# Attention by two pairs of heads: q times the key-value blocks in row halves of TensorE instead of against block-diagonal matrices

## The chip, the cores and the metric

The kernel runs on one core of one Trainium2 chip. The metric is the device time of one execution in microseconds. A core has five engines with their own instruction queues: PE (TensorE, matrix products), DVE (VectorE), ACT (ScalarE), POOL (GpSimd) and SP (here only issuing DMA transfers). PE reads both operands from SBUF and writes to PSUM, which has eight banks of 512 fp32 values in each of 128 partitions. A matrix product is two steps, which the profile shows as two rows: the *stationary* operand (`lhsT`) is loaded (PEld), then the *moving* operand (`rhs`) is streamed past it (PE). `lhsT` has its contraction index on the partitions, and its columns become the output's partitions. All is in fp32; each fp32 product leaves two records in each of the two rows, a transpose leaves one.

## What is computed

Attention without a softmax, normalised by head and followed by a layer of four experts:

```python
kv  = np.einsum('bhsd,bhse->bhde', k, v)          # 64 x 64 per head
out = np.einsum('bhsd,bhde->bhse', q, kv)
rms = np.sqrt(np.mean(out * out, axis=-1, keepdims=True) + 1e-06)
x   = out / rms * g_norm                           # 8 batches, 8 heads, 576 rows, 64
x   = x.transpose(0, 2, 1, 3).reshape(4608, 512)
# experts:
p = domain_probs / (domain_probs.sum(-1, keepdims=True) + 1e-09)
for e in range(4):                                 # w1: 512 x 1024, w2: 1024 x 512
    y += p[:, e:e + 1] * (np.maximum(x @ w1[e], 0.0) @ w2[e])
```

Nearly all arithmetic is in the experts; the kernel computes them by nested Strassen-like forms, which the change does not touch.

## The kernel before

The kernel is written as a plan: every operation is added with a key (where in the program it belongs), an estimated cost by engine, and the buffers it reads and writes. Ahead of time, a list scheduler in the kernel turns this into one fixed order per engine and gives each buffer a slot. So a change of one part moves the order of the others. Attention for batch b+1 is laid between the expert products of batch b, in the first of the four experts; batch 0 comes first, alone. While it runs, PE is given idle transposes of the identity (`idle`, line 1253) wherever the scheduler sees it free.

PSUM's eight banks are in four kinds of two: `u1` and `u2` (first expert product), `db` (second expert product), `ab` (attention). For batch 0, `db` serves attention too.

One batch has eight heads in four pairs. For each pair `hp` (512 of the 576 rows; the remaining 64 rows of all heads follow in one piece):

```python
        def turn(eng, bank=bank, qt=qt):            # line 590: q transposed, two heads on 128 partitions
            for r in range(NR):                     # NR = 4 blocks of 128 rows
                rs = slice(r * P, (r + 1) * P)
                nc.tensor.transpose(bank.ap[:, rs], qt.ap[:, rs], ident[:])
        ...                                         # line 595: ACT copies it to SBUF as qT
        def key_values(eng, bank=bank, kt=kt, vt=vt):   # line 605: two heads in two column halves
            for j in range(KR):                     # KR = 6 pieces of 96 rows
                for r in range(2):
                    nc.tensor.matmul(
                        bank.ap[r * D:(r + 1) * D, 0:D], lhsT=kv_rows(kt)[:, r, j, :],
                        rhs=kv_rows(vt)[:, r, j, :], start=(j == 0), stop=(j == KR - 1),
                    )

        def diagonal(eng, bank=bank, to=kvbd[hp]):  # line 613: into the diagonal of a zeroed 128x128 block
            for r in range(2):
                rows = slice(r * D, (r + 1) * D)
                nc.scalar.activation(out=to.ap[rows, rows], in_=bank.ap[rows, 0:D], func=ACT.Copy)
        ...
        def attend(eng, raw=raw, qT=qT, kb=kvbd[hp]):   # line 623: q times the block-diagonal matrix
            for r in range(NR):
                rs = slice(r * P, (r + 1) * P)
                nc.tensor.matmul(raw.ap[:, rs], lhsT=qT.ap[:, rs], rhs=kb.ap[:])

        plan.add(at(hp + 0.4), pe(4, P), attend, reads=[qT, kvbd[hp]], writes=[raw])
        x = Buf("small", f"x{n}")
        scaled(at(hp + 0.4), n, raw, P, x)
        ...
        def turn_x(eng, bank=bank, x=x):            # line 633: x transposed again, for the experts
            for r in range(NR):
                rs = slice(r * P, (r + 1) * P)
                nc.tensor.transpose(bank.ap[:, rs], x.ap[:, rs], ident[:])
        ...                                         # line 639: ACT copies it, times g_norm
```

With the block-diagonal matrix, one product of 128x128 serves two heads; half of its stationary-by-moving multiplications are with zeros. `scaled` normalises:

```python
    def scaled(key, name, raw, n, x):
        ...
        # line 528, ACT:  sq = raw ** 2                 (n x 512)
        # line 533, DVE:  ss = sum of sq by head        (n x 8)
        # line 538, POOL: ss = ss / 64 + eps
        # line 542, POOL: rt = ss ** -0.5               (n x 8)
        # line 549, DVE:  x = raw * rt                  (n x 512)
```

The remaining 64 rows go through the same steps: transposes (line 657), the product (672), `scaled`, transposes (687):

```python
        def attend_rem(eng):                        # line 672
            for hp in range(NPAIR):
                nc.tensor.matmul(
                    rawr.ap[0:REM, hp * P:(hp + 1) * P], lhsT=qTr.ap[:, hp * REM:(hp + 1) * REM],
                    rhs=kvbd[hp].ap[:],
                )
```

The helper at line 360 is used by all additions of the Strassen-like forms; line 830 is the first expert product, 1044 and 1119 the second in its plain and its deep form, 917 the first product of batch 0.

Of the kernel before, what the change touches and what calls it, by code (L numbers as in the profile page):

```python
# [230 lines left out]
def kernel(  # L231
# [58 lines left out]
    dram = ctx.enter_context(tc.tile_pool(name="dram", bufs=1, space=bass.MemoryType.DRAM))  # L290

    ident = const.tile([P, P], F32, name="ident")
    mhalf = const.tile([P, H], F32, name="mhalf")
    gcol = const.tile([P, 1], F32, name="gcol")
    p_all = const.tile([P, NBLK, E], F32, name="p_all")
    tot = const.tile([P, NBLK], F32, name="tot")
# [2 lines left out]
    BANKS = {"u1": 2, "u2": 2, "db": 2, "ab": 2}  # L299
    SHAPE = {  # L300
        "big": (29, 2 * NT), "w1y": (7, 768), "xf": (5, 2 * NT), "snap": (5, HN),
        "ss": (4, H), "rt": (4, H),
    }
    slots = {
        kind: [
# [209 lines left out]
            halves[c] = [Buf("big", f"x{c}_{dh}") for dh in range(2)]  # L515
        return halves[c]

    def scaled(key, name, raw, n, x):

        sq = Buf("small", f"sq{name}")  # L520
        ss, rt = Buf("ss", f"ss{name}"), Buf("rt", f"rt{name}")

        def rows(b):
            return b.ap[0:n, :].rearrange("p (h d) -> p h d", d=D)

        plan.add(
            key, act(NT),
            lambda eng: nc.scalar.activation(out=sq.ap[0:n, :], in_=raw.ap[0:n, :], func=ACT.Square),
            reads=[raw], writes=[sq],
        )  # L530
        plan.add(
            key, dve(NT),
            lambda eng: nc.vector.reduce_sum(out=ss.ap[0:n, :], in_=rows(sq), axis=AX.X),
            reads=[sq], writes=[ss],
        )

        def power(eng):
            nc.gpsimd.tensor_scalar(
                out=ss.ap[0:n, :], in0=ss.ap[0:n, :], scalar1=1.0 / D, scalar2=EPS,
                op0=ALU.mult, op1=ALU.add,  # L540
            )
            nc.gpsimd.tensor_tensor(
                out=rt.ap[0:n, :], in0=ss.ap[0:n, :], in1=mhalf[0:n, :], op=ALU.pow
            )

        plan.add(key - 0.3, {"POOL": 1.9}, power, reads=[ss], writes=[ss, rt])
        plan.add(
            key, dve(NT),
            lambda eng: nc.vector.tensor_tensor(
                out=rows(x), in0=rows(raw),  # L550
                in1=rt.ap[0:n, :].unsqueeze(2).to_broadcast([n, H, D]), op=ALU.mult,
            ),
            reads=[raw, rt], writes=[x],
        )

    def attention(b, key, span, rem):

        kvbd = {}
        at = lambda j: key + span * j / (NPAIR + 1)
        for hp in range(NPAIR):  # L560
            hs = slice(2 * hp, 2 * hp + 2)
            n = f"{b}_{hp}"
            kind = "kv" if b or hp < 2 else "big"
            kt, vt, qt = Buf(kind, f"k{n}"), Buf(kind, f"v{n}"), Buf("small", f"q{n}")
            want = at(hp) - 0.25 if b else key - 1 + 0.1 * hp

            def kv_rows(t):
                return t.ap[0:KP, 0:2 * KR * D].rearrange("p (h j d) -> p h j d", h=2, d=D)

            for r in range(2):  # L570
                load(
                    want, qt,
                    lambda qt=qt, r=r: qt.ap[:].rearrange(
                        "p (r h d) -> p r h d", h=2, d=D)[:, :, r, :],
                    q[b, 2 * hp + r, 0:NT, :].rearrange("(p r) d -> p r d", r=NR), 128,
                )
            for t, src in ((kt, k), (vt, v)):
                load(
                    want, t,
                    lambda t=t: t.ap[0:KP, 0:2 * KR * D].rearrange("p (h x) -> p h x", h=2),  # L580
                    src[b, hs].rearrange("h (p j) d -> p h (j d)", j=KR), 288,
                )

            bank = Buf("ab", f"qT{n}")
            qT = Buf("small", f"qT{n}")

            def turn(eng, bank=bank, qt=qt):
                for r in range(NR):
                    rs = slice(r * P, (r + 1) * P)
                    nc.tensor.transpose(bank.ap[:, rs], qt.ap[:, rs], ident[:])  # L590

            plan.add(at(hp), pe(4, P, 1), turn, reads=[qt], writes=[bank])
            plan.add(
                at(hp), act(NT),
                lambda eng, bank=bank, qT=qT: nc.scalar.activation(
                    out=qT.ap[:], in_=bank.ap[:], func=ACT.Copy),
                reads=[bank], writes=[qT],
            )
            bank = Buf("ab" if b else "ab", f"kv{n}")
            kvbd[hp] = Buf("kvbd", f"kvbd{n}")  # L600

            def key_values(eng, bank=bank, kt=kt, vt=vt):
                for j in range(KR):
                    for r in range(2):
                        nc.tensor.matmul(  # L605
                            bank.ap[r * D:(r + 1) * D, 0:D], lhsT=kv_rows(kt)[:, r, j, :],
                            rhs=kv_rows(vt)[:, r, j, :], start=(j == 0), stop=(j == KR - 1),
                        )

            def diagonal(eng, bank=bank, to=kvbd[hp]):  # L610
                for r in range(2):
                    rows = slice(r * D, (r + 1) * D)
                    nc.scalar.activation(out=to.ap[rows, rows], in_=bank.ap[rows, 0:D], func=ACT.Copy)

            plan.add(at(hp), {"PE": 0.87}, key_values, reads=[kt, vt], writes=[bank])
            plan.add(at(hp), {"ACT": 0.5}, diagonal, reads=[bank], writes=[kvbd[hp]])

            raw = Buf("ab" if b else "db", f"raw{n}")

            def attend(eng, raw=raw, qT=qT, kb=kvbd[hp]):  # L620
                for r in range(NR):
                    rs = slice(r * P, (r + 1) * P)
                    nc.tensor.matmul(raw.ap[:, rs], lhsT=qT.ap[:, rs], rhs=kb.ap[:])  # L623

            plan.add(at(hp + 0.4), pe(4, P), attend, reads=[qT, kvbd[hp]], writes=[raw])
            x = Buf("small", f"x{n}")
            scaled(at(hp + 0.4), n, raw, P, x)
            bank = Buf("ab" if b else "db", f"xT{n}")

            def turn_x(eng, bank=bank, x=x):  # L630
                for r in range(NR):
                    rs = slice(r * P, (r + 1) * P)
                    nc.tensor.transpose(bank.ap[:, rs], x.ap[:, rs], ident[:])  # L633

            plan.add(at(hp + 1), pe(4, P, 1), turn_x, reads=[x], writes=[bank])
            xh = x_halves(b)[hp // 2]
            plan.add(
                at(hp + 1), act(NT),
                lambda eng, bank=bank, xh=xh, kt=hp % 2: nc.scalar.activation(
                    out=xh.ap[:, kt * NT:(kt + 1) * NT], in_=bank.ap[:], func=ACT.Copy,  # L640
                    scale=gcol[:]),
                reads=[bank], parts=[xh],
            )

        n = f"{b}_r"
        at = lambda j: rem + 0.1 * (j - NPAIR)
# [18 lines left out]
            lambda eng: nc.scalar.activation(out=qTr.ap[:, 0:HN], in_=tb.ap[:, 0:HN], func=ACT.Copy),  # L665
            reads=[tb], writes=[qTr],
        )
        rawr = Buf("ab", f"raw{n}")

        def attend_rem(eng):  # L670
            for hp in range(NPAIR):
                nc.tensor.matmul(  # L672
                    rawr.ap[0:REM, hp * P:(hp + 1) * P], lhsT=qTr.ap[:, hp * REM:(hp + 1) * REM],
                    rhs=kvbd[hp].ap[:],
                )

        plan.add(
            at(NPAIR), pe(4, P), attend_rem, reads=[qTr] + [kvbd[hp] for hp in range(NPAIR)],
            writes=[rawr],
        )  # L680
        xr = Buf("small", f"x{n}")
        scaled(at(NPAIR), n, rawr, REM, xr)
        xb = Buf("ab", f"xT{n}")

        def turn_xrem(eng):
# [571 lines left out]
    with tc.manual_schedule(engines={ENG.PE, ENG.DVE, ENG.Activation, ENG.Pool, ENG.SP}):  # L1257
        for i in range(P // D):
            nc.sync.dma_start(out=gcol[i * D:(i + 1) * D, :], in_=g_norm.unsqueeze(1))
        make_identity(nc, ident[:])  # L1260
        nc.vector.memset(mhalf[:], -0.5)
        nc.vector.memset(bd_home[:], 0.0)
        held = None
        wide = {}
        for op in order:
            if op.seed:
                bank, n = op.marks
                assert wide.get((bank.kind, bank.slot), 0) >= n, "a seed would be overwritten"
            elif op.eng == "PE":
                for b in op.outs:  # L1270
                    wide[b.kind, b.slot] = op.marks[1] if op.marks else 0
            made = op.fn(op.eng)
            if op.port and op.eng == "DVE":
                held = made.ins.name
            elif op.port and op.eng == "POOL" and held is not None:
                tc.add_manual_dep(made.ins, held, mybir.DependencyInfo(
                    mybir.DependencyClass.Sync, mybir.DependencyReason.DATA
                ), reason="SBUF port")
# [28 lines left out]
```

## Time and profile before

The time is 1748.28 us, the median of three runs (1747.76 to 1748.77). The profiled execution spans 1747.1 us. PE's clock is granted in full throughout.

| | PE | PEld | DVE | ACT | POOL |
|---|---|---|---|---|---|
| busy, us | 1738.6 | 1664.1 | 1151.4 | 931.6 | 719.7 |
| instructions | 14222 | 14222 | 1712 | 2274 | 758 |

What attention leaves in the trace:

| line | engine | what | records | length of one, ns |
|---|---|---|---|---|
| 590, 633 | PE | transposes of q and of x, 128x128 | 128 and 128 | 272 to 273 |
| 605 | PE | keys times values, 96x64 by 96x64 | 768 | 222 |
| 623 | PE | q times the block-diagonal, 128x128 | 256 | 275 |
| 672 | PE | the same for the remaining rows | 64 | 273 |
| 1253 | PE | idle transposes at the start | 94 | 273 to 325 |
| 595 | ACT | copy of the transposed q | 32 | 597 |
| 613 | ACT | copy of a diagonal block | 64 | 219 |
| 528 | ACT | squares | 40 | 597 |
| 533 | DVE | sums by head | 40 | 685 |
| 538, 542 | POOL | scale, power | 40 and 40 | 197, 1636 |
| 549 | DVE | multiply | 40 | 690 |
| 639 | ACT | copy of x, times g_norm | 32 | 688 |

How to read it: PE's records overlap, [...]so the length of one says little of what it costs. What it costs is the distance from its start to the start of the next. A record of PEld is likewise longer than the distance to the next load.

### The profile page before, as it was taken

The page shows a single profiled execution, that of the slowest core. Times are in us where ns is not written, and L with a number is a line of the kernel's source. Part 1 is how long each engine was busy: PE and PEld are TensorE (multiplying, and loading weights), DVE is VectorE, ACT ScalarE, POOL GpSimd, SP SyncE. Part 2 cuts the span into 40 slices and gives each one's busy share as a digit, 9 for nine tenths or more (in the row PEclk, how much of TensorE's full clock was granted, in tenths as well). Part 3 has the DMA queues.
Part 4 walks back from the last instruction along what each step waited for, and adds up shares of the span by engine and source line. Part 5 has one row for each costly group of instructions (what it writes and reads, how often), then busy time and mean ns, then how long its engine had stood idle before and what let it go on. Part 6 is the DMA issues. An engine that isn't in the chain of part 4 may idle for free.

```text
span 1747.1 us, 36218 instructions
## 1 busy us (share of the span) xinstructions
PE 1738.6 (100%) x14222; PEld 1664.1 (95%) x14222; DVE 1151.4 (66%) x1712; ACT 931.6 (53%) x2274; POOL 719.7 (41%) x758
## 2 busy tenths in 40 slices
PE   9999999999999999999999999999999999999998
PEld 7699999999999999999999999999999999999997
DVE  4854554555565567777786567777787567777774
ACT  3454544554444456666555456665655446666662
POOL 2534343444233424333355624333345624333331
PEclk9999999999999999999999999999999999999999
DMA  9765444533343334444456434444456434444442
GB/s 230 237 185 180 136 144 139 147 128 119 120 146 100 103 98 110 109 109 110 122 158 156 101 94 112 107 109 110 109 158 169 109 90 108 117 108 110 107 103 49
DMA packets 148587, 220.80 MB, mean 126 GB/s; under 512 B 49600, under 2 KB 90816, under 8 KB 148416
## 3 DMA queue, kind: packets, MB, share of 16 engines
q1 hardware_dynamic: 133312, 191.21, 35.2%
q0 software_dynamic: 15104, 27.27, 11.3%
q8 instruction: 112, 1.84, 0.4%
q14 instruction: 59, 0.48, 0.1%
HBM read 145.30 MB, written 73.14 MB: 125 GB/s over the span
## 4 chain that ended last, share of the span: by engine, by line
PE 99%; DMA 0%; DVE 0%; ACT 0%; SPq 0%; issue 0%; ACTq 0%
PE u L830 44%; PE db L1044 17%; PE db L1119 16%; PE ab L1119 10%; PE ab L1044 4%; PE u L917 2%; PE ab L605 2%; PE ab L623 1%; PE ab L590 1%; PE ab L633 1%; PE ab L1253 1%; PE ab L672 0%; DMA small<-in_q_dram 0%; PE db L623 0%; PE ab L687 0%; PE ab L657 0%
## 5 line engine op out<-in xcount | busy, mean ns | idle before, releaser
L360 DVE TENSOR_TENSOR big<-big,big 128x1024 f32<-128x1024 f32 (+1 forms) x429 | 479.1, 1128 | 61.9 <-ACT big L813 33.4
L830 PE MATMUL u<-xf,big 128*128 128x128 f32 x3536 | 508.4, 275 | 0.0
L830 PEld LDWEIGHTS u<-xf,big 128*128 128x128 f32 x3536 | 455.5, 192 | 4.8 <-issue 0.9
L830 PE MATMUL u<-xf,w1y 128*128 128x128 f32 x2652 | 381.3, 275 | 0.0
L857 DVE TENSOR_TENSOR big<-u,snap 128x256 f32<-128x256 f32 x446 | 188.1, 422 | 254.6 <-PE u L830 170.9
L830 PEld LDWEIGHTS u<-xf,w1y 128*128 128x128 f32 x2652 | 342.8, 192 | 3.9
L849 ACT ACTIVATE snap<-u 128x256 f32<-128x256 f32 x490 | 187.9, 383 | 249.0 <-PE u L830 211.5
L1044 PE MATMUL db<-big,big 128*128 128x256 f32 x1192 | 280.2, 380 | 0.0
L1044 PEld LDWEIGHTS db<-big,big 128*128 128x128 f32 x1192 | 216.3, 190 | 24.5 <-issue 0.2
L849 ACT ACTIVATE big<-u 128x256 f32<-128x256 f32 x446 | 170.0, 383 | 95.7 <-PE u L830 63.0
L360 POOL TENSOR_TENSOR big<-big,big 128x256 f32<-128x256 f32 (+1 forms) x116 | 139.4, 1217 | 111.6 <-DVE big L360 75.1
L360 POOL TENSOR_TENSOR big<-big 128x512 f32<-128x512 f32 (+1 forms) x78 | 93.0, 1194 | 169.0 <-DVE big L360 120.6
L813 ACT ACTIVATE big<-big 128x1024 f32<-128x1024 f32 x124 | 130.2, 1052 | 8.8 <-DVE big L360 7.0
L1185 POOL TENSOR_TENSOR big<-big 128x512 f32<-128x512 f32 x19 | 24.1, 1270 | 217.9 <-DVE big L360 164.1
L1119 PE MATMUL db<-big,big 128*128 128x128 f32 x788 | 113.0, 275 | 0.0
L1147 ACT ACTIVATE snap<-db 128x256 f32<-128x256 f32 (+1 forms) x168 | 60.0, 357 | 94.5 <-PE db L1119 87.2
L849 ACT ACTIVATE u<-u 128x256 f32<-128x256 f32 x245 | 91.0, 372 | 25.9 <-PE u L830 10.2
L1119 PEld LDWEIGHTS db<-big,big 128*128 128x128 f32 x788 | 100.3, 192 | 0.0
L1014 POOL DMA_DIRECT2D out_dram<-big x98 | 88.3, 987 | 22.4 <-ACT big L991 16.6
L991 ACT ACTIVATE big<-db,p_all 128x256 f32<-128x256 f32 x90 | 42.6, 473 | 95.1 <-PE db L1044 93.9
L1119 PE MATMUL db<-kv,big 128*128 128x128 f32 x624 | 88.6, 275 | 0.0
L1119 PE MATMUL ab<-kv,big 128*128 128x128 f32 x588 | 84.1, 275 | 0.0
(200 smaller groups left out, 2687.1 us busy)
## 6 DMA issues: line engine op xcount, KB each, us to landing
xf<-x SPq DMA_DIRECT2D x108, 512.0 KB, 3.6
out_dram<-big POOLq DMA_DIRECT2D x82, 256.0 KB, 5.5
xf<-x_h SPq DMA_DIRECT2D x81, 256.0 KB, 3.2
xf<-x SPq DMA_DIRECT2D x81, 256.0 KB, 3.4
x<-xf SPq DMA_DIRECT2D x36, 512.0 KB, 3.3
big<-in_moe_w_dram SPq DMA_DIRECT2D x28, 512.0 KB, 4.9
small<-in_q_dram SPq DMA_DIRECT2D x72, 128.0 KB, 4.0
kv<-in_k_dram SPq DMA_DIRECT2D x30, 288.0 KB, 3.5
```

Source lines behind the costliest of these rows:

```text
L360: lambda eng: adder(eng).tensor_tensor(out=out_(), in0=a(), in1=b(), op=op),
L605: nc.tensor.matmul(bank.ap[r * D:(r + 1) * D, 0:D], lhsT=kv_rows(kt)[:, r, j, :], rhs=kv_rows(vt)[:, r, j, :], start=(j == 0), stop=(j == ...
L813: lambda eng: nc.scalar.activation(out=b.ap[:], in_=b.ap[:], func=ACT.Relu),
L830: nc.tensor.matmul(ps.ap[:, u * P:(u + 1) * P], lhsT=w1f[e][m][mm][1]()[:, u * P:(u + 1) * P], rhs=views[m][mm][1](), start=(mm in (1, 5) ...
L849: lambda eng: nc.scalar.activation(out=where(), in_=ps.ap[:, 0:HN], func=ACT.Copy),
L857: lambda eng: nc.vector.tensor_tensor(out=block(whole, a, t), in0=src.ap[:, 0:HN], in1=add_.ap[:], op=ALU.add),
L917: nc.tensor.matmul(bank.ap[:], lhsT=two(w.ap[:])[:, kt, ut * P:(ut + 1) * P], rhs=two(xh[dh].ap[:])[:, kt, :], start=(dh == kt == 0), stop ...
L991: lambda eng: nc.scalar.activation(out=cell(i, half), in_=ap(), func=ACT.Copy, scale=prob()),
L1014: nc.gpsimd.dma_start(out=dst, in_=cell(i)[parts, :], accum_op=ALU.add)
L1044: nc.tensor.matmul(ps.ap[:, 0:HN], lhsT=four(h[m])[:, kt // 2, t, kt % 2, :], rhs=w2f[e][m].ap[:, kt * HN:(kt + 1) * HN], start=(m in (1, ...
L1119: nc.tensor.matmul(ps.ap[:, o * P:(o + 1) * P], lhsT=b.ap[:, col:col + P], rhs=w2q[e][m][mm][1]()[:, kt, :], start=(mm in (1, 5) and o == ...
L1147: lambda eng: nc.scalar.activation(out=where(), in_=group_of(ps.ap), func=ACT.Copy),
```

## The change

The change takes two pairs of heads together (a group) and does without block-diagonal matrices. The key-value blocks of a group's four heads lie in one bank and are copied by one ACT instruction as they are: the two heads of a pair above each other on 128 partitions, the pairs side by side. q times a key-value block is then done head by head: a head's 64 partitions of the transposed q are the stationary operand, its 64x64 block the moving one. The even heads use the upper 64 rows of PE, the odd heads the lower 64, and each parity writes to a bank of its own (`raw[0]`, `raw[1]`). The products with zeros go. `scaled` squares and multiplies bank by bank, and sums and takes the power of both at once (16 sums a row in place of 8); its second multiply puts the heads back in their order by a strided output. The normalised rows of a group are in a buffer of 1024 columns.

```diff
-            def diagonal(eng, bank=bank, to=kvbd[hp]):
-                for r in range(2):
-                    rows = slice(r * D, (r + 1) * D)
-                    nc.scalar.activation(out=to.ap[rows, rows], in_=bank.ap[rows, 0:D], func=ACT.Copy)
...
+                def key_values(eng, bank=kbank, kt=kt, vt=vt, o=o):
+                    for j in range(KR):
+                        for r in range(2):
+                            nc.tensor.matmul(
+                                bank.ap[r * D:(r + 1) * D, o * D:(o + 1) * D],
+                                lhsT=kv_rows(kt)[:, r, j, :], rhs=kv_rows(vt)[:, r, j, :],
+                                start=(j == 0), stop=(j == KR - 1), skip_group_check=True,
+                            )
...
             plan.add(
+                at(2 * g + 1), act(P),
+                lambda eng, bank=kbank, to=kv[g]: nc.scalar.activation(
+                    out=to.ap[:], in_=bank.ap[:, 0:P], func=ACT.Copy),
+                reads=[kbank], writes=[kv[g]],
+            )
+            raw = [Buf("ab" if b > 1 else "db", f"raw{b}_{g}_{r}") for r in range(2)]
...
-            def attend(eng, raw=raw, qT=qT, kb=kvbd[hp]):
-                for r in range(NR):
-                    rs = slice(r * P, (r + 1) * P)
-                    nc.tensor.matmul(raw.ap[:, rs], lhsT=qT.ap[:, rs], rhs=kb.ap[:])
-
-            plan.add(at(hp + 0.4), pe(4, P), attend, reads=[qT, kvbd[hp]], writes=[raw])
+            def attend(eng, raw=raw, g=g):
+                for o in range(2):
+                    for i in range(NR):
+                        for r in range(2):
+                            half = slice(r * D, (r + 1) * D)
+                            nc.tensor.matmul(
+                                raw[r].ap[:, (o * NR + i) * D:(o * NR + i + 1) * D],
+                                lhsT=qTs[2 * g + o].ap[half, i * P:(i + 1) * P],
+                                rhs=kv[g].ap[half, o * D:(o + 1) * D],
+                            )
+
             plan.add(
+                at(2 * g + 1.4), {"PE": 1.0}, attend, reads=[qTs[2 * g], qTs[2 * g + 1], kv[g]],
+                writes=raw,
+            )
+            x = Buf("big", f"xg{b}_{g}")
+            scaled(at(2 * g + 1.4), f"{b}_{g}", raw, P, x, 2 * NR)
...
         def attend_rem(eng):
             for hp in range(NPAIR):
-                nc.tensor.matmul(
-                    rawr.ap[0:REM, hp * P:(hp + 1) * P], lhsT=qTr.ap[:, hp * REM:(hp + 1) * REM],
-                    rhs=kvbd[hp].ap[:],
-                )
+                for r in range(2):
+                    half = slice(r * D, (r + 1) * D)
+                    nc.tensor.matmul(
+                        rawr[r].ap[0:REM, hp * D:(hp + 1) * D],
+                        lhsT=qTr.ap[half, hp * REM:(hp + 1) * REM],
+                        rhs=kv[hp // 2].ap[half, hp % 2 * D:(hp % 2 + 1) * D],
+                    )
...
-        nc.vector.memset(bd_home[:], 0.0)
```

Not shown: `scaled`, which now runs over two banks as told above (its buffer of squares is gone; the squares go into x's own buffer), and the sizes of its small buffers (two of 16 columns in place of four of 8).

## The prediction, made before the changed kernel ran

> **What bounds the kernel now.** I read the page from the top: busy shares, then the chain of work that ended last, then the waits of PE.
>
> ```profile
> PE 1738.6 (100%) x14222; PEld 1664.1 (95%) x14222; DVE 1151.4 (66%) x1712; ACT 931.6 (53%) x2274; POOL 719.7 (41%) x758
> ...
> PE 99%; DMA 0%; DVE 0%; ACT 0%; SPq 0%; issue 0%; ACTq 0%
> ```
>
> The first line gives busy time and instruction counts by engine, the second the chain's shares of the span. PE, the matmul row, has work in 1738.6 of 1747.1 us and carries 99% of the chain; the other engines have a third of their time or more to spare. In the waits of PE only four single entries appear (1.4, 1.1, 0.8 and 0.4 us). So a change is worth what it changes in PE's own time, whatever it does for DVE, ACT or GpSimd, unless it makes PE wait.
>
> "Busy" here hides how fast matmuls follow each other: a record of a 128-column product lasts 275 ns, but the next starts long before. So the rate must be read from starts. The timeline of PE around one key-value block (start, length, engine, line, count of records):
>
> ```profile
> 155.31 0.50 PE L830 MATMUL u<-xf,big 128*128 128x128 f32 x3
> 155.74 0.92 PE L605 MATMUL ab<-kv,kv 96*64 96x64 f32 x24
> 156.59 0.46 PE L657 MATMUL ab<-ident,small 64*128 64x64 f32 x4
> 156.98 1.16 PE L830 MATMUL u<-xf,w1y 128*128 128x128 f32 x8
> 157.97 1.06 PE L623 MATMUL ab<-kvbd,small 128*128 128x128 f32 x8
> 158.87 0.38 PE L1044 MATMUL db<-big,big 128*128 128x256 f32 x1
> ```
>
> and of its weight loads (the stationary operand, lhsT):
>
> ```profile
> 155.74 0.78 PEld L605 LDWEIGHTS ab<-kv,kv 96*64 96x64 f32 x24
> ...
> 157.86 0.97 PEld L623 LDWEIGHTS ab<-kvbd,small 128*128 128x128 f32 x8
> ```
>
> Three rates come out. An fp32 matmul is two records. (a) L623, the q product that the change rewrites: 8 records from 157.97 to 158.87, 0.90 us for one pair of heads, **112 ns a record**. (b) L605, two products in two column halves of PE: 0.92 us less the 222 ns of one record, over 23 gaps, is **30 ns a record**, though each streams 64 columns; (a)'s rate would give 56. So two halves do run side by side. (c) Entering such a stretch costs: the last L830 record starts at 155.31+0.50-0.275 = 155.535, the next is 0.205 later instead of 0.11; leaving L605 takes 0.15 instead of 0.03. **About 0.1 us for each change of mode**, 0.2 for an excursion. L623 pays none of it now, since its neighbours are 128x128 too. The remainder's product L672 does:
>
> ```profile
> 161.58 1.09 PE L672 MATMUL ab<-kvbd,small 128*64 128x128 f32 x8
> 162.60 0.71 PE L830 MATMUL u<-xf,big 128*128 128x128 f32 x4
> ```
>
> It takes 1.02 us from its start to the next.
>
> [...]loads of 128 columns last 192 ns (L623), of 64 columns 138 (L605), 54 ns apart for 64 columns.[...]
>
> **The change part by part.** *The q product.* Before, two pairs of heads are 2 x 0.90 = 1.80 us, 16 times in the kernel: 28.8 us. After, two pairs are 16 products of half the rows and half the moving columns, 32 records. If the moving columns set the pace as in L605, 32 x 30 ns = 0.97 us. But L605's stationary operand has 64 columns; here it is still a q block of **128 columns**, and there are twice as many loads. [...]If the two halves load side by side, two records take about 112 ns, 16 x 0.112 = 1.79 us, plus 0.2 for the excursion: 1.99. Nothing is gained in the halving, and the excursion is lost: 16 x 0.19 = **+3.0 us**.
>
> *The remainder's q product* has 64-column weights, so L605's rate fits: 16 records x 30 ns = 0.48, plus 0.2, is 0.68 against 1.02, 8 times: **-2.7 us**.
>
> *The start.* Before the first feed-forward product PE has little to do and the program puts in idle transposes of the identity (L1253). They stand on PE's queue and take its time whether needed or not. There are 94 such records in the trace; the order of the changed program has 120, because a group of two pairs must be complete before its q product and the second group's now stands ahead of the first feed-forward product. 26 x 0.111 = **+2.9 us**.
>
> *The chain behind the q product.* For two pairs: two squares on ACT (0.60 each), a row sum of 1024 on DVE (0.69 now for 512, so about 1.2), POOL's scale (0.2) and power, two multiplies on DVE (0.69 each). The power took 1.64 us for 8 columns; 16 columns take 1.64 to 3.3. That is 5.6 to 7.3 us, some 0.4 more with hand-overs. In the changed order PE has 6.2 us of work between the first q product and the transpose that needs its result (40 records of transposes at 0.11 and two key-value blocks of 0.86), 7.8 behind the second, and over 8 from then on. So only the first can stall PE, by 0 to 1.5 us: **+0.5**.
>
> *Off the path:* eight copies of a diagonal block (0.22 us each on ACT) become two of 128 columns per batch, the row sums are fewer, the zeroing of the block-diagonal buffer (0.91 us on DVE while PE waits for q) goes. ACT, DVE and POOL are not the bound, so these are worth nothing. Key-value products, transposes and everything of the feed-forward part keep their counts, and the last 2499 rows of PE's order are the same.
>
> Sum: 3.0 - 2.7 + 2.9 + 0.5 = +3.7, so **1752 us**.
>
> **The rivals.** (1) *The moving columns set the pace after all.* Then a group is 0.97 + 0.2 = 1.17 us and the q products save 16 x 0.63 = 10.1; with -2.7 and +3.4 the sum is -9.4: 1739 us. For it: L605's rate. Against it: 54 ns of load per 64 columns; L605 cannot tell[...].
> (2) *Row halves do not load side by side.* Then each record waits for a full load, 32 x 0.11 + 0.2 = 3.7 us a group, +30 us; the remainder gains nothing (16 x 54 ns + 0.2); with the start +34: 1782 us. For it: no row half beside another in this trace. Against it: column halves do it.
> (3) *A half cannot load while it multiplies itself.* [...]L605 speaks against it.
> (4) *PSUM or the chain becomes a wait.* In the later batches a q product holds both banks of the attention pair until the second multiply, some 6 to 8 us. The eight batches stretch over some 400 us (L623 runs from 12.6 to 396.5), near 50 each, and PE has other products to go on with, so I expect no more than 2 us.
>
> **Range and chances.** I give the main case about one half, rival 1 a fifth, rivals 2 and 3 three in ten together. 1737 to 1780 holds the first, the main case and most of the others. All but the far end of rival 2 lie within 2% of 1748.28 (1713 to 1783), so "same" is nearly sure.
>
> **What would show it.** In the changed timeline: the 32 records of one q product, start to next start. 1.9 to 2.1 us confirms the load as the pace, 1.1 to 1.2 rival 1,[...] 3.5 or more rival 2. The remainder's should take about 0.7. The idle transposes should number 120 and the first feed-forward product start 1 to 3 us after 25.87. The waits of PE should stay under 5 us; a large one on the multiply or the transpose's copy would mean rival 4. The prediction is wrong if row halves share loads in a way that the column halves do not show, or if the power on 16 columns holds up more than the first group.

## The result and the profile after

The changed kernel takes 1751.77 us (1751.34 to 1752.37), against 1748.53 us for the kernel before (four runs, one more than above): 3.2 us more, a ratio of 1.0019 with a 95% interval of 1.0001 to 1.0036. The difference is small, and the interval only just excludes 1. The products with zeros, half of all in that step, are gone for nothing.

The page of the changed kernel, busy time and instructions by engine, then the chain's shares:

```profile
PE 1741.5 (100%) x14568; PEld 1663.4 (95%) x14568; DVE 1154.8 (66%) x1745; ACT 917.7 (52%) x2234; POOL 702.0 (40%) x684
...
PE 99%; DMA 0%; DVE 0%; SPq 0%; ACT 0%; issue 0%
```

PE is still the chain. Its busy time rose by 2.9 us, as the span did by 3.1 (1747.1 to 1750.2). ACT lost 14 us and POOL 18, which moved nothing.

The timeline of PE around one q product of a group (start, length, engine, line, count of records). L866 is the first expert product, L649 the q product:

```profile
136.72 0.61 PE L866 MATMUL u<-big,w1y 128*128 128x128 f32 x4
137.26 2.00 PE L649 MATMUL ab<-kvbd,small 64*128 64x64 f32 x32
139.20 0.71 PE L866 MATMUL u<-big,big 128*128 128x128 f32 x4
```

From 137.26 to 139.20 are 1.94 us. Within the stretch the records stand (2.00 - 0.272)/31 = **56 ns** apart, 111 ns for the two halves. Entering costs 0.1 more: the last L866 record starts at 136.72+0.61-0.275 = 137.055, and the first of L649 comes 0.205 later, where another of L866 would come 0.11 later. So a group costs 2.03 us where the block-diagonal form cost 1.80. The remainder's product of the same kernel is the counter-example:

```profile
167.32 1.89 PE L1080 MATMUL db<-big,big 128*128 128x256 f32 x8
169.14 0.68 PE L710 MATMUL ab<-kvbd,small 64*64 64x64 f32 x16
169.75 0.48 PE L1080 MATMUL db<-big,big 128*128 128x256 f32 x1
```

It too uses two row halves and streams 64 columns, but its stationary operand has 64 columns in place of 128: (0.68 - 0.218)/15 = **31 ns** a record. Same moving columns, same halves, half the columns to load, and 31 ns in place of 56. That already points at the load, and it rules out that records of the q product wait 56 ns merely to be issued.

### The profile page after: what moved, and what is told of

The parts are those of the page before. It is cut to its first block, busy times and chain, and to the rows that moved or that the text cites. A ratio compares the mean times of both kernels' runs of the same rounds, so it can differ in the third digit from the quotient of the medians.

```text
span 1750.2 us, 36758 instructions
## 1 busy us (share of the span) xinstructions
PE 1741.5 (100%) x14568; PEld 1663.4 (95%) x14568; DVE 1154.8 (66%) x1745; ACT 917.7 (52%) x2234; POOL 702.0 (40%) x684
## 4 chain that ended last, share of the span: by engine, by line
PE 99%; DMA 0%; DVE 0%; SPq 0%; ACT 0%; issue 0%
PE u L866 44%; PE db L1080 17%; PE db L1155 16%; PE ab L1155 10%; PE ab L1080 4%; PE u L953 2%; PE ab L629 2%; PE ab L649 1%; PE ab L616 1%; PE ab L1289 1%; PE ab L668 1%; PE db L649 0%; PE ab L710 0%; DMA small<-in_q_dram 0%; PE db L668 0%; PE ab L693 0%
## 5 line engine op out<-in xcount | busy, mean ns | idle before, releaser
L866 PE MATMUL u<-xf,big 128*128 128x128 f32 x3536 | 509.3, 275 | 0.0
L360 DVE TENSOR_TENSOR big<-big,big 128x1024 f32<-128x1024 f32 (+1 forms) x420 | 464.2, 1117 | 56.1 <-ACT big L849 26.0
L866 PEld LDWEIGHTS u<-xf,big 128*128 128x128 f32 x3536 | 456.1, 192 | 4.3
L866 PE MATMUL u<-xf,w1y 128*128 128x128 f32 x2652 | 383.0, 276 | 0.0
L866 PEld LDWEIGHTS u<-xf,w1y 128*128 128x128 f32 x2652 | 342.1, 192 | 3.8
L1080 PE MATMUL db<-big,big 128*128 128x256 f32 x1192 | 280.4, 380 | 0.0
L1080 PEld LDWEIGHTS db<-big,big 128*128 128x128 f32 x1192 | 216.3, 190 | 24.5
L360 POOL TENSOR_TENSOR big<-big,big 128x256 f32<-128x256 f32 (+1 forms) x125 | 161.1, 1303 | 162.3 <-DVE big L360 64.8
```

Of the source, the lines that this page charges most:

```text
L360: lambda eng: adder(eng).tensor_tensor(out=out_(), in0=a(), in1=b(), op=op),
L866: nc.tensor.matmul(ps.ap[:, u * P:(u + 1) * P], lhsT=w1f[e][m][mm][1]()[:, u * P:(u + 1) * P], rhs=views[m][mm][1](), start=(mm in (1, 5) ...
L1080: nc.tensor.matmul(ps.ap[:, 0:HN], lhsT=four(h[m])[:, kt // 2, t, kt % 2, :], rhs=w2f[e][m].ap[:, kt * HN:(kt + 1) * HN], start=(m in (1, ...
```

## The experiments

Theory A: the load of the 128-column stationary operand sets the pace of the q product, the two row halves load side by side, and each change of mode (from products on all of PE to products on halves of it, or back) costs PE 0.1 us. Rival B: the streaming of the moving columns sets it. Rival C: a limit on how fast records can be issued, whatever they do. All times below are medians with their ratio to the kernel before, which ran beside each. The changed kernel's 1751.8 was measured at another time, so the spans of the profiled runs are given too where such a difference matters.

### Twice the moving columns

```diff
-                                raw[r].ap[:, (o * NR + i) * D:(o * NR + i + 1) * D],
+                                raw[r].ap[:, min(o * NR + i, 6) * D:min(o * NR + i, 6) * D + P],
-                                rhs=kv[g].ap[half, o * D:(o + 1) * D],
+                                rhs=kv[g].ap[half, 0:P],
```

> The changed kernel, with 128 moving columns in each half-row q product in place of 64 (both pairs' key-value blocks; the results overlap in PSUM, so the output is not the reference's). If the load of the 128-column stationary operand sets the pace[...]: the q product stays at 1.9 to 2.0 us for a group and the time within 2 us of 1751.8. If the stream sets the pace, or load and stream follow each other within a half, the records go from 56 to 80 ns or more apart: 16 x 32 x 25 ns = at least 13 us more, 1765 or above.

1754.08 us, ratio 1.0032 (1.0020 to 1.0044): its interval overlaps that of the changed kernel, though the median is 2.3 us above, a little more than the 2 us that I had allowed. The profiled span is 0.6 us longer (1750.8 against 1750.2). Its timeline:

```profile
137.37 2.06 PE L649 MATMUL ab<-kvbd,small 64*128 64x128 f32 x32
139.35 0.71 PE L866 MATMUL u<-big,big 128*128 128x128 f32 x4
```

1.98 us from start to start in place of 1.94. Twice the columns cost a group 0.04 us, or 0.6 us in sixteen. So in the changed kernel the stream was not the pace. A half also loads its next operand while it streams: two records take 2 x (2.06 - 0.272)/31 = 115 ns, while 128 columns stream in about 108 (an estimate from L1080 above: eight products of 256 columns, each record 0.380 us long, stand (1.89 - 0.380)/7 = 216 ns apart) and a load into one half takes 99 by the next experiment. Rival B falls, and with it the third rival of the prediction. Rival C is not touched by this run.

### One half at a time

```diff
-                for o in range(2):
-                    for i in range(NR):
-                        for r in range(2):
+                for r in range(2):
+                    for o in range(2):
+                        for i in range(NR):
```

> The changed kernel, with the order of the sixteen q products of a group changed: first the eight of the even heads (upper row half), then the eight of the odd heads. Nothing else is different. If the two halves load side by side only because their products alternate, [...]32 x 0.11 = 3.5 us a group in place of 1.8, 16 x 1.75 = +28 us, 1780. If the 56 ns of a record is instead the rate of a load or of the issue, whichever half it goes to, nothing changes: 1752.

1788.09 us, ratio 1.0231 (1.0216 to 1.0246). The timeline of one group and the loads of that line:

```profile
122.54 3.39 PE L649 MATMUL ab<-kvbd,small 64*128 64x64 f32 x32
125.86 0.71 PE L866 MATMUL u<-xf,w1y 128*128 128x128 f32 x4
```

```profile
122.54 3.25 PEld L649 LDWEIGHTS ab<-kvbd,small 64*128 64x128 f32 x32
```

With the same instructions in another order a record takes (3.39 - 0.272)/31 = 101 ns instead of 56, though it streams 64 columns as before. The loads stand (3.25 - 0.188)/31 = 99 ns apart: that is a load of 128 columns into one half, measured by itself. The order alone changes the time, so it matters which half a record goes to, and the 56 ns of the changed kernel come from two such loads side by side. A limit on issue that does not look at the halves can't give the 101 ns, and it isn't behind the 56 ns either, since the remainder's records stand 31 ns apart: rival C falls.

This accounts for 16 x (3.32 - 1.94) = 22 us, but the profiled run is 40 us longer than the changed kernel's (1790.3 against 1750.2). The rest is in the clock. The windows of this run, one from an earlier dip of the clock and three just after the stretch above (window, its length, busy time with records for PE, PEld, DVE, ACT and POOL, then the granted PE clock, DMA share and GB/s):

```profile
21.00:24.00 3.00, 3.00 (x32) 2.55 (x31) 1.03 (x1) 0.00 (x0) 1.79 (x2) 0.50 1.04 386
...
123.00:126.00 3.00, 3.00 (x31) 2.93 (x31) 1.30 (x2) 0.63 (x2) 0.00 (x0) 1.00 0.78 238
126.00:129.00 3.00, 3.00 (x17) 3.00 (x18) 1.82 (x2) 1.33 (x3) 1.01 (x2) 0.57 0.94 271
129.00:132.00 3.00, 3.00 (x16) 2.61 (x16) 0.00 (x0) 0.68 (x2) 2.47 (x1) 0.86 1.12 337
```

PE is busy in every window, and its granted clock falls to half (0.50 from 21 to 24 us, a window that lies whole within a dip). The dip after the stretch above takes 1.29 + 0.42 = 1.71 us (0.57 and 0.86 of 3 us each), which at 0.50 is 3.4 us long. There are nine dips in the first 420 us; one of them (34.3 to 41.1 us) lasts twice as long, so that ten times 1.71 = 17 us are lost. 1750.2 + 22 + 17 = 1789, against a span of 1790.3. The other three runs, with 0.992 to 0.993 of the clock granted in place of 0.990, span 1784.7 to 1785.9. My expectation of 1780 had the rate and knew nothing of the clock.

### Four quarters

```diff
-                        for r in range(2):
+                        for r, c in ((0, 0), (1, 1), (0, 1), (1, 0)):
                             half = slice(r * D, (r + 1) * D)
                             nc.tensor.matmul(
-                                raw[r].ap[:, (o * NR + i) * D:(o * NR + i + 1) * D],
-                                lhsT=qTs[2 * g + o].ap[half, i * P:(i + 1) * P],
+                                raw[r].ap[c * D:(c + 1) * D, (o * NR + i) * D:(o * NR + i + 1) * D],
+                                lhsT=qTs[2 * g + o].ap[half, i * P + c * D:i * P + (c + 1) * D],
```

> The changed kernel, with each half-row q product cut again into two of 64 stationary columns, so that four quarters of PE alternate (64 products of 64x64 a group... 32 products, 64 records; the result is the same). Load theory: [...]four records could take 60 ns: 64 x 15 = 1.0 us a group, 16 x 0.85 = -14 us, 1738. Rival: records cannot follow each other faster than the 30 ns of the key-value products, whatever they load: 64 x 30 = 1.9 us, and the time stays at 1752. If the quarters of one row half don't load side by side it is 64 x 30 or slower too, up to 64 x 55: 1778.

1743.87 us, ratio 0.9972 (0.9961 to 0.9983), the first version below the kernel before.

```profile
133.88 1.16 PE L649 MATMUL ab<-kvbd,small 64*64 64x64 f32 x64
134.97 0.71 PE L866 MATMUL u<-big,big 128*128 128x128 f32 x4
```

Twice as many records in little more than half the time: (1.16 - 0.218)/63 = **15 ns** a record, 60 ns for the four quarters. 1.09 us instead of 1.94 a group is 13.6 us for sixteen; the profiled run is 11.8 us shorter than the changed kernel's, the medians differ by 7.9. The single runs lie between 1740.2 and 1745.1, and why most are longer than the profiled one the traces do not tell. The issue limit of 30 ns, which I held possible, does not exist at this level.

### The key-value products of a group in one stretch

```diff
-                plan.add(at(hp), {"PE": 0.87}, key_values, reads=[kt, vt], parts=[kbank])
+                if b == 0:          # batch 0 as before
+                    ...
+                elif o == 0:
+                    first, held = key_values, [kt, vt]
+                else:               # one plan step: both pairs' products behind each other
+                    plan.add(at(hp), {"PE": 1.6}, both, reads=held + [kt, vt], writes=[kbank])
```

> The changed kernel, with the key-value products of a group's two pairs directly behind each other on PE, for batches 1 to 7 (batch 0 as it was). Nothing is computed differently. If entering and leaving a mode costs PE 0.1 us each, fourteen excursions of 0.2 us go: -2.8 us, 1749. If what looked like the cost of a mode is a latency that other work fills, or the wait for both pairs' loads holds PE up, the time stays at 1752 or rises.

1749.04 us, ratio 1.0009 (1.0001 to 1.0018), 2.7 us below the changed kernel. The two ratios' intervals overlap, but all twelve runs (1748.30 to 1750.83) lie below the fastest of the changed kernel's four (1751.34), and the profiled spans differ by 2.8 us.

```profile
130.55 1.62 PE L629 MATMUL ab<-kv,kv 96*64 96x64 f32 x48
132.10 0.71 PE L875 MATMUL u<-xf,big 128*128 128x128 f32 x4
```

Two pairs take 1.55 us to the next start, where one pair takes 0.85. With the entry (0.1) the merger saves 0.25, fourteen times: 3.5 us by the timeline, of which 2.8 show in the span. So most of what looks like the cost of a change of mode is real time of PE, and can be saved by placing like beside like.

### The remainder's part alone, in the kernel before

```diff
-                nc.tensor.matmul(
-                    rawr.ap[0:REM, hp * P:(hp + 1) * P], lhsT=qTr.ap[:, hp * REM:(hp + 1) * REM],
-                    rhs=kvbd[hp].ap[:],
-                )
+                for r in range(2):
+                    half = slice(r * D, (r + 1) * D)
+                    nc.tensor.matmul(
+                        (rawr, rawo)[r].ap[0:REM, hp * D:(hp + 1) * D],
+                        lhsT=qTr.ap[half, hp * REM:(hp + 1) * REM], rhs=kvbd[hp].ap[half, half],
+                    )
```

(with squares and multiplies over the two banks.)

> The kernel before, with only the product of the remaining 64 rows by row halves (64 stationary and 64 moving columns, a second bank for the odd heads); pairs and block-diagonal products stay for the rest. By the prediction's sum this part alone is worth 8 x (1.02 - 0.70) = -2.6 us: 1745.3 where before is 1747.9, with 94 idle transposes as before. If the gain is eaten by the second bank (the attention banks are two) or by the longer ACT and DVE steps, it stays at 1748.

1753.72 us, ratio 1.0033 (1.0020 to 1.0045): slower by 6 us, not faster by 2.6. The product itself is as expected: 0.61 us from start to start (171.17 to 171.78). The time went elsewhere, as the timeline of PE shows at its two longest stalls (in brackets the idle time before and who ended it):

```profile
79.91 1.12 PE L678 MATMUL ab<-ident,small 128*128 128x128 f32 x4 [1.73 <-DVE small L549]
...
90.96 1.16 PE L668 MATMUL ab<-kvbd,small 128*128 128x128 f32 x8 [2.16 <-DVE small L593]
```

In the first, transposes of x wait for the multiply of their own pair (L549), which is late in the new order. In the second, the next q product waits for a bank: the remainder now holds both attention banks until its multiply (L593) is done. From 78 to 87 us, around the end of the first stall, the granted clock of this run was 0.78, 0.50 and 0.58 in three windows of 3 us, up to 3.4 us lost; what lowered it is not shown. The changed kernel's remainder takes two banks too, and there PE's list of waits has none on a multiply; what in its order spares it is not shown. As a test of the sum's second term it failed, because it changed the waits as well.

### The start

First, batch 0's transposes of x into the attention banks:

```diff
-                bank = Buf("ab" if b > 1 else "db", f"xT{b}_{hp}")
+                bank = Buf("ab" if b != 1 else "db", f"xT{b}_{hp}")
```

> The changed kernel, with batch 0's transposes of x going to the attention banks, so that the second group's q product need not wait until the first group's two db banks are copied out. Bank theory: that q product starts at about 24.6 us in place of 26.9, the fourteen idle transposes between go, and the start is 2 us shorter: 1749.8. Chain theory: the second group's chain of some 7 us behind its q product then lies open ahead of the products that need it, idle transposes come there instead (116 in all in place of 120), and the gain is 0.4 us: 1751.3.

1754.77 us, ratio 1.0039 (1.0027 to 1.0052). The second group's q product started at 25.88 in place of 26.90, though the first one was 0.5 us later than in the changed kernel because q landed later. The first feed-forward product gained only 0.5 us (28.30 in place of 28.83), 18 idle transposes then stood behind the second group's q product in place of 8, and the feed-forward product after the first sixteen records came at 38.95 in place of 38.93. So the bank theory of the start falls, and the chain theory fits: what the start needs is the second group's chain. The new order also brought a wait of 1.8 us at 80 us, which is most of the 2.4 us by which the span is longer (1752.6 against 1750.2):

```profile
80.02 1.99 PE L1080 MATMUL db<-big,big 128*128 128x256 f32 x8 [1.84 <-DVE big L560]
```

Second, no idle transposes at all (the scheduler's limit set ahead of the start):

```diff
-    order = plan.layout(slots, later, idle, ("ab", "db"), 0.0)
+    order = plan.layout(slots, later, idle, ("ab", "db"), -9.0)
```

> The changed kernel without the 120 idle transposes at the start. If their time is taken from useful work, the first feed-forward product starts up to 3 us earlier than 28.8 us. If the start is bound by the loads and by the chain of the first group, they only fill: it starts at 27 to 29 us all the same. And if PE's clock depends on how busy its array is, as the run with one half at a time suggests (0.99 granted over the whole span), the clock then falls in the first 40 us and the time rises by 2 to 6 us, to 1754 to 1758.

1758.33 us, ratio 1.0057 (1.0041 to 1.0072).

```profile
15.65 3.68 PE L649 MATMUL db<-kvbd,small 64*128 64x64 f32 x32
...
26.48 1.94 PE L668 MATMUL db<-ident,big 128*128 128x128 f32 x8 [3.15 <-DVE big L560]
...
32.80 9.88 PE L953 MATMUL u<-big,big 128*128 128x512 f32 x16
```

The same 32 records take 3.68 us in place of 2.00. The 24 records of a key-value product (L629) take 1.55 in place of 0.92 up to 21.79, and the first sixteen of the feed-forward product (L953) 9.88 in place of 7.13; from 42.52 on, eight transposes take 1.04 again, as in the changed kernel. So PE runs at little more than half its rate until some way into L953. (The clock column reads 1.00 there all the same; what lowers the rate is not shown.) So the first feed-forward product came at 32.80, 4 us later than with idle transposes, and not at 27 to 29 as I expected of loads and chain alone. And even without idle transposes PE waits 3.15 us for the first group's multiply. The idle transposes fill waits that the group's chain imposes, and with them PE is at its full rate at the first q product (2.00 us from 15.14).

### Putting the gains together

Four quarters, key-value products in one stretch, and the bank of the first experiment on the start:

> The changed kernel with the three parts together: q products in four quarters (measured -8 us), the key-value products of a group in one stretch from batch 1 on (-2.7), batch 0's transposes of x in the attention banks (114 idle transposes in place of 120). If they add up: 1751.8 - 8 - 2.7 - 0.6 = 1740.5. If the quarters' gain in the profile (11.8 us of span) is the real one, 1737. If one of them brings PE waits that the others hid, above 1742.

1745.63 us, ratio 0.9989 (0.9981 to 0.9997). The parts do not add up. The largest waits of PE (who waited for whom, us in total, times, longest):

```profile
PE ab L616 <- DVE big L560: 2.7, 5, 0.5
...
PE ab L616 <- DVE small L560: 2.0, 4, 0.8
```

The transposes of q (L616) wait for an attention bank that the group's multiply (L560) has yet to free. The scheduler placed them by its estimate of 2.1 us for scale and power, while the trace of the changed kernel has

```profile
19.61 0.20 POOL L547 TENSOR_SCALAR ss<-ss 128x16 f32<-128x16 f32 x1 [18.31 <-DVE ss L540]
19.89 2.94 POOL L551 TENSOR_TENSOR rt<-ss,mhalf 128x16 f32<-128x16 f32 x1
```

Two more versions without the change of the start gave the plan 3.3 us for this step and 1.2 us for the q product, from batch 1 on:

```diff
-        plan.add(key - 0.3, {"POOL": 2.1}, power, reads=[ss], writes=[ss, rt])
+        plan.add(key - 0.3, {"POOL": 3.3 if blocks > NPAIR and name[0] != "0" else 2.1}, power, ...)
-                at(2 * g + 1.4), {"PE": 1.0}, attend, ...
+                at(2 * g + 1.4), {"PE": 1.2 if b else 1.0}, attend, ...
```

With four quarters alone (and these costs):

> The version with four quarters, in which the plan's costs are set to what the traces show from batch 1 on: 3.3 us for scale and power of 16 columns on GpSimd (in place of 2.1) and 1.2 us for a q product (in place of 1.0). Only the order of instructions changes. The profile of the four quarters has no PE wait after the start, so nothing should be gained: 1743.9 within 1.5 us. If waits that its profile did not show make its other runs longer than the profiled one, it falls towards 1740.

1742.51 us, ratio 0.9968 (0.9956 to 0.9979), the same as without within the intervals. With four quarters and the key-value products in one stretch:

> Four quarters and the key-value products of a group in one stretch, with the true costs in the plan, and batch 0 as in the changed kernel. In the combination before, PE waited nine times (4.7 us) for a bank that the multiply of the group had still to free, as the plan had the power 1.1 us too short. If that is the cause, these waits go and the parts add up: 1743.9 - 2.7 = 1741.2. If the waits come from having both pairs' loads and two banks taken at once, whatever the plan knows of the power, they stay: 1745.6.

**1741.10 us, ratio 0.9962 (0.9949 to 0.9976)**, the best of all. The nine waits of q's transposes for the multiply are gone from its list of waits. Its interval overlaps that of the four quarters alone. So it is likely, but not shown, that the key-value products still add something on top. And as costs and start changed together against the combination before, the gain over it is not split between them.

## Why the prediction was right, step by step

The time was 1751.8 where 1752 was predicted. The mechanism of the q product was the one predicted; the start cost what was predicted for another reason, and the sizes come out so. The start and the chain are read from these lines, the first feed-forward product of the kernel before:

```profile
25.87 1.88 PE L917 MATMUL u<-big,big 128*128 128x512 f32 x4
```

and in the changed kernel the squares and multiplies (L533, L560) of the first group, the transposes of its x (L668), and the first feed-forward product:

```profile
17.18 1.09 ACT L533 ACTIVATE big<-db 128x512 f32<-128x512 f32 x2 [1.33 <-PE db L649]
...
22.87 1.29 DVE L560 TENSOR_TENSOR big<-db,rt 128x512 f32<-128x512 f32 x2 [3.35 <-POOL rt L551]
...
24.41 1.04 PE L668 MATMUL db<-ident,big 128*128 128x128 f32 x8
...
28.83 7.13 PE L953 MATMUL u<-big,big 128*128 128x512 f32 x16
```

The terms:

- *The q product*, +3.0: 2.03 us a group, entry included, against 1.80 is +0.23, sixteen times +3.7. That the load sets the pace and the halves load side by side is shown by the runs with twice the columns (1.98 us a group against 1.94), with one half at a time (101 ns a record against 56) and with quarters (15). The load of 128 columns into one half took 99 ns.
- *The remainder*, -2.7: the step compared unlike things. It counted both changes of mode in the new form and only the leaving in the old, whose 1.02 us run from its start. With entry the old is 1.11, the new 0.61 + 0.1 = 0.71: -3.2. Doing this part alone did not confirm the sum, as told.
- *The start*, +2.9: the first feed-forward product came at 28.83 in place of 25.87, +2.96, with 120 idle transposes. But about 0.5 of the 2.96 is the two dearer q products ahead of it, which the first term has already. And the prediction took the idle transposes themselves for the cost, while they are the sign of the longer chain: from the end of the q product to the end of the second multiply it takes 7.02 us with them (17.14 to 24.16). Without them the transposes that wait for that multiply start 7.15 us after the q product's end (19.33 to 26.48), and PE stands idle for 3.15 of it.
- *The chain*, +0.5: the power took 2.94 us, inside the stated 1.6 to 3.3, and the first transpose of x (24.41) found its input ready, by 0.25 us. It did so partly because PE had waited 0.69 us just before (at 20.95) for a copy of the transposed q, which is already in the start's +2.96. As a term of its own it is 0.
- *PSUM as a wait* (rival 4): PE's listed waits are 4.0 us against 3.7 before, so it did not happen here. It did happen when the three parts were put together, and in the kernel before with two banks for the remainder.

Sum of the corrected terms, with 0.5 off for what the start and the first term share: 3.7 - 3.2 + 2.9 - 0.5 = +2.9, against +3.1 in the spans. That the median came within 0.3 us of the prediction is luck: the sum of +3.7 was 0.7 too low for the q product, and 0.5 too high each for the remainder, the overlap and the chain, and the runs of either kernel spread over 1 us or more.

## What to carry to other kernels

A product has two operands to bring in, and halving one does not help if the other sets the pace: here half the moving columns and half the rows left the load of 128 stationary columns as it was, once per half (99 ns each). Ask for each product how long its load is against its stream, cut the longer one (the quarters did, 111 to 60 ns), and place products of one mode together, as each change of mode cost 0.1 us. When several steps become faster, an estimate in the plan that is 1 us short may begin to matter: the nine waits of the first combination were gone with the costs as traced, though that version had the old start as well.

## What the runs showed of the hardware that I had not expected

With one row half in use at a time, for 3.3 us a stretch, PE's granted clock fell to half for some 3.4 us nine times in sixteen stretches (once for twice as long), although the profile shows PE busy throughout. With 0.50 as their depth, the windows of 3 us put the starts of the nine dips at 20.64, 34.26, 64.98, 82.08, 99.12, 126.42, 286.86, 351.72 and 416.58 us, each to about 0.03. The distances from the first are 4, 13, 18, 23, 31, 78, 97 and 116 times 3.413 us, to within 0.04. Three stretches whose place the timelines give can be laid against that grid. Of those from 61.90 and from 122.54, 3.1 and 2.8 us fall into the one interval of 3.41 us that ends where the dip begins. The one from 158.47 to 161.79 straddles the grid's point at 160.57, with 2.1 us before it and 1.2 behind, and no dip follows (1.00 in every window from 132 to 285 us). So where a stretch lies on the grid may decide; three stretches do not settle it. Whether the unused row half brings the dips, or the records of 64 columns that stand 101 ns apart (56 in the changed kernel, whose profiled run shows no dip), is not shown either. It was seen in one order of one kernel only.

Four quarters ran at 15 ns a record, each with its own load of 64 columns and its own 64 moving columns, 60 ns for four. As 64 columns more made a load 54 ns longer in the kernel before (192 against 138), this fits four loads side by side. GpSimd's power cost 1.64 us on 8 columns and 2.94 on 16, 1.8 times as long.
